# A two-layer decode kernel on one core: the last matmuls kept company by idle products, and one ninth of the gate's rows moved to 64 partitions and eight short transfers

## The chip, the core and the metric

The kernel runs on one NeuronCore of a Trainium2 chip. The metric is the device time of one execution in microseconds; the figure for a kernel is the median of several runs.

## What is computed

One token of two sequences (B = 2, model width D = 576) goes through attention over a cache, a gated MLP, the same attention once more and the same MLP once more. All arrays are float32, and both layers use the same weights and caches.

```python
B, Sq, D = 2, 1, 576
H, Sk, Dh = 32, 8192, 128          # k_cache, v_cache: (B, H, Sk, Dh)
Df = 4608                          # w_gate, w_up: (D, Df); w_down: (Df, D)
x = A_x
x = x + attention(layernorm(x))    # softmax(q k^T / sqrt(Dh)) v, then wo
x = x + mlp(layernorm(x))          # (gelu(x w_gate) * (x w_up)) w_down
x = x + attention(layernorm(x))
x = x + mlp(layernorm(x))
```

Each cache has 2 x 32 x 8192 x 128 values of 4 bytes, 268 MB in the units of the profile, and is read once per layer, apart from a few heads that stay in place from the first layer to the second. The three MLP matrices have 10.6 MB each and are read in both layers.

## The kernel before, in words

All loads go out from one engine, SyncE (SP in the profile), in an order that is written down in Python before any arithmetic: `plan_first`, `plan_mlp(0)`, `plan_second` and `plan_mlp(1)` append closures to one `queue`, and `pump` issues from its head as long as the head finds room. The room is one tile, `space`, of 50,176 float32 per partition, handed out by `Arena`. `done(key)` is called in the code behind the products that used a piece; it frees the piece's stretch and pumps again. The framework keeps eight semaphores for SP's transfers and goes round them, so that a transfer is issued only when the one eight places before it has landed; it may also wait for the engines that read its place before.

Attention (`attention`) goes over 62 items, each one batch and one or two heads: VectorE and GpSimd multiply the keys by the query, VectorE adds up, ScalarE makes the softmax, and TensorE multiplies by the values. In the second layer it goes through the items backwards and ends with eight pieces of `wo` (`project`, `out_rows`).

What the change touches is the second MLP, `mlp(1)`. Its weights are laid out as half rows. `half_rows` reads a matrix of 576 rows as 1152 half rows of 2304 values; partition p holds the nine half rows 9p to 9p + 8, called u = 0 to 8. A piece `us` of several u is one transfer. `GU` gives the pieces: before, the gate has three pieces of three u each (3456 KB a piece), the up matrix two pieces of three and three of one (1152 KB). `norm` lays the normalised x, transposed, in the tile `xt`, in nine blocks of 32 columns, block u matching half row u, with six columns of padding in front, so that `window(u, at)` can cut out eight columns of a block with the wanted columns shifted. `all_products` (L849) then accumulates for each u, each v of two and each c of four one product with 8 columns of `xt` held and 288 columns of weights moved.

`activate` (L858 to L871) turns the accumulated gate and up halves into `hT`: ScalarE, VectorE and again ScalarE in a chain of some ten small steps, once for v = 0 and once for v = 1. Behind it stand the products with the down matrix (L884). `DOWN[1]` gives its pieces: three of nine rows i (2592 KB), t = 0, 1 and 2, and the last nine rows, t = 3, as pieces of 3, 3, 2 and 1 (864, 864, 576, 288 KB). Each row i costs four products of 144 columns. In the records of the profile a float32 product appears twice, so that a nine-row piece has 72 records. `add_to_x` (L495) adds the sum to `x`, and four small transfers, two from SP and two from ScalarE's queue (L897), each of two partitions of 576 bytes, write the output.

Of the kernel before, what the change touches and what calls it, by code (L numbers as in the profile page):

```python
# [15 lines left out]
P = 128  # L16
# [24 lines left out]
NPLACE = 4  # L41
RING = 5 * SLOT
END = RING + NPLACE * PLACE
HELD = 5


# [76 lines left out]
def decode_layers(ctx, tc, x_in, kc, vc, wq, wo, wg, wu, wd, out):  # L123
# [97 lines left out]
    def half_rows(key, w, us, first):  # L221
# [6 lines left out]

        weights(key, len(us) * width, first, transfers)

    def split_rows(name, w, h, u):

        rows = w[:, DF // 2 * h:DF // 2 * (h + 1)].rearrange("(m r) w -> m r w", r=NU)

        def transfers(t):
            for e in range(2):
                nc.sync.dma_start(t[e::2, :], rows[:, 5 * e + u, :])

        weights((name, 0, h, u), DF // 2, None, transfers)
# [39 lines left out]
    def out_rows(layer, g):  # L279
# [12 lines left out]
    single = [range(u, u + 1) for u in range(NU)]  # L292
    three = [range(u, u + 3) for u in range(0, NU, 3)]
    WQ = [three, single]
    GU = [three, three[:-1] + single[-3:]]

    DOWN = [
        [[(t, i) for i in range(lo, lo + 4)] for t in range(NT) for lo in (0, 4)] + [[(t, NI - 1) for t in range(NT)]],
        [[(t, i) for i in range(NI)] for t in range(NT - 1)]
        + [[(NT - 1, i) for i in range(lo, hi)] for lo, hi in ((0, 3), (3, 6), (6, 8), (8, 9))],  # L300
    ]

    whole_at = (None, 0)
    def groups(layer):
# [70 lines left out]
    def plan_mlp(layer):  # L375
        if layer == 0:
            for h in range(2):
                for u in range(4):
                    split_rows("g", wg, h, u)
                split_middle(h)  # L380
                for u in range(4):
                    split_rows("u", wu, h, u)
        else:
            for g, (name, w) in enumerate((("g", wg), ("u", wu))):
                for us in GU[g]:
                    half_rows((name, layer, us[0]), w, us, 0)
        for rows in DOWN[layer]:
            down(layer, rows)

# [20 lines left out]
    diag = consts.tile([P, 4], F32, name="diag")  # L410
    of = consts.tile([P, B], F32, name="of")
    both = ident.rearrange("p (c v b r) -> p b r v c", c=4, v=4, b=B)[:, :, :, 0, :]
    eight = consts.tile([P, B, 4], F32, name="eight")
    nc.vector.reduce_sum(eight, both, axis=AX.X)
    nc.vector.tensor_add(diag, eight[:, 0, :], eight[:, 1, :])
    nc.vector.reduce_sum(of, eight, axis=AX.X)
# [18 lines left out]

    xt = consts.tile([P, PAD + NU * 32], F32, name="xt")
    nc.vector.memset(xt, 0.0)


# [17 lines left out]
        return smalls[0][0:p, 0:n]  # L459


    def norm(split=False):
        stats = work.tile([P, 6], F32, name="stats")
        nc.vector.bn_stats(stats, x)
        apart = work.tile([P, 4, 6], F32, name="apart")
        nc.vector.tensor_mul(
            apart, stats.unsqueeze(1).to_broadcast([P, 4, 6]), strip.unsqueeze(2).to_broadcast([P, 4, 6])
        )
        every4 = small(P, 4 * 6)
        nc.tensor.matmul(every4, same, apart.rearrange("p c t -> p (c t)"), start=True, stop=True)  # L470
        mv = work.tile([P, 2], F32, name="mv")
        nc.vector.bn_aggr(mv, every4)
        xc = once.tile([P, CW, 2], F32, name="xc", tag="xc")
        xr = x.rearrange("p (m r) -> p r m", r=NU)
        xs = xc.rearrange("p w s -> p (w s)")
        if split:
            xm = xs[:, :5 * 32].rearrange("p (u m e) -> p u m e", u=5, e=2)
            parts = [(xm[:, 0:4, :, e], xr[:, 5 * e:5 * e + 4, :], 0) for e in range(2)]
            parts += [(xm[:, 4, :, e], xr[:, 4, :], e) for e in range(2)]
            xs = xs[:, :5 * 32].rearrange("p (u q) -> p u q", u=5)  # L480
        else:
            parts = [(xc[:, :, s], x, s) for s in range(2)]
            xs = xs.rearrange("p (q u) -> p u q", u=NU)
        for to, of_x, s in parts:
            nc.vector.tensor_scalar(to, of_x, mv[:, 0:1], side[:, s:s + 1], op0=ALU.subtract, op1=ALU.mult)
        u = xs.shape[1]
        nc.vector.transpose(xt[:, PAD:PAD + 32 * u].rearrange("p (u q) -> p u q", u=u), xs)
        ve = work.tile([P, 1], F32, name="ve")
        nc.vector.tensor_scalar_add(ve, mv[:, 1:2], EPS)  # L489
        rstd = work.tile([P, 1], F32, name="rstd")  # L490
        nc.gpsimd.tensor_tensor(out=rstd, in0=ve, in1=mhalf, op=ALU.pow)  # L491
        return rstd
# [5 lines left out]
    def attention(layer):  # L498
# [314 lines left out]
            project(g)  # L813
        add_to_x()


    def mlp(layer):
        split = layer == 0
        rstd = norm(split)
        hT = once.tile([P, 2, NI, 2, 2, B], F32, name="hT", tag="xc")  # L820

        def window(u, at):

            return xt[:, PAD + 32 * u - at:PAD + 32 * u - at + 4 * B]

        def split_products(h):

            steps = [(("g", layer, h, u), u, 2, (0,)) for u in range(4)] + [(("gu", layer, h), 4, 1, (0, 1))]
            steps += [(("u", layer, h, u), u, 2, (1,)) for u in range(4)]
            for key, u, sides, gs in steps:  # L830
                w = ready.pop(key).rearrange("p (k c w) -> p k c w", c=4, w=HG)
                for k in range(2):
                    g, e = (k, 0) if u == 4 else (gs[0], k)
                    for c in range(4):
                        nc.tensor.matmul(  # L835
                            acc[32 * c:32 * c + 4 * B, h, :HG], window(u, 4 * g + 2 * e), w[:, k, c, :],
                            start=(key == steps[0][0] and k == 0), stop=(key == steps[-1][0] and k == 1),
                        )
                done(key)

        def all_products():

            for g, name in enumerate("gu"):
                for us in GU[g]:
                    w = ready.pop((name, layer, us[0])).rearrange("p (u v c w) -> p u v c w", v=2, c=4, w=HG)
                    for u in us:
                        for v in range(2):
                            for c in range(4):
                                nc.tensor.matmul(  # L849
                                    acc[32 * c:32 * c + 4 * B, v, :HG], window(u, 4 * g), w[:, u - us[0], v, c, :],  # L850
                                    start=(g == 0 and u == 0), stop=(g == 1 and u == NU - 1),
                                )
                    done((name, layer, us[0]))

        def activate(v):

            o = once.tile([P, 2, HG], F32, name="o", tag="row")
            nc.scalar.activation(o[:, 0, :], acc[:, v, :HG], AF.Copy, scale=rstd)  # L858
            gu = o[:, 1, :].rearrange("p (i r) -> p i r", i=NI)
            nc.vector.transpose(gu, o[:, 0, :].rearrange("p (m i) -> p i m", i=NI))  # L860
            g = gu[:, :, 0:4]
            a = once.tile([P, NI, 4], F32, name="ga", tag="part")
            nc.vector.tensor_mul(a, g, g)
            nc.vector.tensor_scalar(a, a, 0.044715, 1.0, op0=ALU.mult, op1=ALU.add)
            nc.vector.tensor_mul(a, a, g)
            nc.scalar.activation(a, a, AF.Tanh, scale=math.sqrt(2.0 / math.pi))
            nc.vector.scalar_tensor_tensor(a, a, 1.0, g, op0=ALU.add, op1=ALU.mult)
            nc.vector.tensor_mul(a, a, gu[:, :, 4:8])
            a, to = a.rearrange("p i (e b) -> p (i e) b", b=B), hT[:, v].rearrange("p i e s b -> p (i e) s b")
            nc.vector.tensor_scalar_mul(to[:, :, 0, :], a, 0.5)  # L870
            nc.scalar.mul(to[:, :, 1, :], a, 0.5)  # L871

        if not split:
            all_products()
        for v in range(2):
            if split:
                split_products(v)
            activate(v)
        for rows in DOWN[layer]:
            w = ready.pop(("d", layer, rows[0])).rearrange("p (i c) -> p i c", c=D)  # L880
            for k, (t, i) in enumerate(rows):
                v, e = divmod(t, 2) if split else (t % 2, t // 2)
                for c in range(4):
                    nc.tensor.matmul(  # L884
                        xps[32 * c:32 * c + 2 * B, :], hT[:, v, i, e, :, :].rearrange("p s b -> p (s b)"),
                        w[:, k, c * CW:(c + 1) * CW],
                        start=(rows is DOWN[layer][0] and k == 0), stop=(t, i) == (NT - 1, NI - 1),
                    )
            done(("d", layer, rows[0]))
        add_to_x()  # L890
# [2 lines left out]
    mlp(0)  # L893
    attention(1)
    mlp(1)
    for c in range(4):
        (nc.sync, nc.scalar)[c % 2].dma_start(  # L897
            out[:, :, c * CW:(c + 1) * CW].rearrange("b s d -> (b s) d"), x[32 * c:32 * c + B, :]
        )


# [25 lines left out]
```

## Time and profile before

| what | value |
|---|---|
| time, median of 3 runs | 2692.36 us (2692.12 to 2692.72) |
| time of the profiled execution | 2692.03 us |
| its span, first to last instruction | 2690.2 us |
| TensorE, VectorE, GpSimd busy | 917.2, 1851.0, 1213.9 us |
| bytes read from the chip's memory | 1153.18 MB |

All times inside the execution are microseconds from the start of the span. The span is 1.83 us shorter than the profiled execution's own time, and this execution was 0.33 us faster than the median. In a timeline row the first number is the start, the second the length from the first to the last instruction of the group, and the bracket says how long the engine had been idle before and what ended that. PE is TensorE, PEld its loads of held operands, DVE VectorE, ACT ScalarE, SPq and ACTq the issue of transfers from SyncE and ScalarE. In a row of stretches stand, for each engine, its busy time and its count of instructions, then the granted share of TensorE's clock, the mean busy share of the 16 DMA engines and what they moved in GB/s; a packet counts in the stretch in which it starts.

### The profile page before, as it was taken

How to read it: one execution, taken by the hardware profiler on the slowest of the kernel's cores; microseconds unless marked ns; L12 is line 12 of the kernel's file. 1: busy time of each engine (PE TensorE's matmuls, PEld its weight loads, DVE VectorE, ACT ScalarE, POOL GpSimd, SP SyncE). 2: the span in 40 equal slices, each digit the busy share in tenths (PEclk: the TensorE clock that was granted, in tenths of full speed). 3: DMA queues.
4: the chain of work that ended last, by engine and by line, in shares of the span. 5: the costliest groups of instructions: out<-in, count | busy, mean ns of one | idle time of the engine just before them, and what ended most of it. 6: DMA issues, size and time to landing. Idle time of an engine off the chain costs nothing.

```text
span 2690.2 us, 18178 instructions
## 1 busy us (share of the span) xinstructions
PE 917.2 (34%) x7020; PEld 300.9 (11%) x7020; DVE 1851.0 (69%) x1688; ACT 144.6 (5%) x736; POOL 1213.9 (45%) x550
## 2 busy tenths in 40 slices
PE   1323332332233233334654332233233323332355
PEld 0100010000001010111211110001010101010022
DVE  4877787678777776867028777777776877787740
ACT  0000000000000000000016000000000000000000
POOL 2644454454445444544018454445444544454420
PEclk7656656665666566666666665666566556656677
DMA  9999999999999999999999999999999999999998
GB/s 421 435 437 433 427 436 430 434 436 430 436 432 433 431 431 434 435 427 425 406 402 419 436 435 431 435 432 433 433 433 433 432 434 432 434 433 431 434 423 378
DMA packets 33687, 1154.36 MB, mean 429 GB/s; under 512 B 4008, under 2 KB 4032, under 8 KB 5824
## 3 DMA queue, kind: packets, MB, share of 16 engines
q1 hardware_dynamic: 33560, 1153.19, 99.7%
q8 instruction: 55, 0.90, 0.1%
q14 instruction: 32, 0.26, 0.0%
q10 hardware_dynamic: 40, 0.01, 0.0%
HBM read 1153.18 MB, written 0.00 MB: 429 GB/s over the span
## 4 chain that ended last, share of the span: by engine, by line
DMA 79%; PE 11%; DVE 7%; POOL 1%; ACT 1%; issue 1%; SPq 0%; ACTq 0%; POOLq 0%; DVEq 0%
DMA space<-in_A_k_cache_dram 40%; DMA space<-in_A_v_cache_dram 32%; PE acc L672 10%; DVE space L557 5%; DMA space<-in_B_w_down_dram 2%; DVE S L577 2%; DMA space<-in_B_w_gate_dram 2%; DMA space<-in_A_wo_dram 1%; DMA space<-in_B_w_up_dram 1%; POOL space L574 1%; DMA space<-in_A_wq_dram 1%; PE bank L884 0%; ACT space L567 0%; PE acc L835 0%; POOL space L561 0%
## 5 line engine op out<-in xcount | busy, mean ns | idle before, releaser
L574 POOL TENSOR_TENSOR space<-space 128x1024 f32<-128x1024 f32 (+1 forms) x510 | 1180.6, 2315 | 1207.8 <-DVE space L557 1197.0
L557 DVE TENSOR_TENSOR space<-space,bank 128x2048 f32<-128x2048 f32 (+1 forms) x512 | 1153.6, 2253 | 607.7 <-DMA space<-in_A_k_cache_dram 573.8
L672 PE MATMUL acc<-space,prz 128*8 128x512 f32 x4096 | 590.9, 740 | 451.9 <-DMA space<-in_A_v_cache_dram 447.8
L577 DVE TENSOR_REDUCE S<-space 128x16 f32<-128x1024 f32 (+1 forms) x512 | 609.8, 1191 | 3.5 <-POOL space L574 3.3
L525 PE MATMUL bank<-qsb,pick 4*64 4x128 f32 (+1 forms) x256 | 46.9, 439 | 780.2 <-DVE space L557 777.6
L672 PEld LDWEIGHTS acc<-space,prz 128*8 128x8 f32 x4096 | 118.5, 104 | 867.3 <-DMA space<-in_A_v_cache_dram 449.0
L629 ACT ACTIVATE nbs<-bank 64x1 f32<-64x1 f32 (+1 forms) x128 | 21.1, 165 | 2254.3 <-PE bank L608 2253.6
L525 PEld LDWEIGHTS bank<-qsb,pick 4*64 4x64 f32 (+1 forms) x256 | 21.1, 203 | 838.9 <-DVE space L557 807.7
L697 PE MATMUL bank<-of,osb 128*32 128x2 f32 x512 | 40.9, 202 | 130.8 <-DVE osb L688 130.8
L608 PE MATMUL bank<-m,unit 1*128 1x2 f32 (+1 forms) x136 | 39.2, 355 | 129.1 <-DVE m L606 129.1
L491 POOL TENSOR_TENSOR rstd<-ve,mhalf 128x1 f32<-128x1 f32 x4 | 2.2, 550 | 167.6 <-DVE ve L489 167.6
L688 DVE SCALAR_TENSOR_TENSOR osb<-acc,diag,osb 128x128 f32<-128x128 f32 x192 | 67.3, 351 | 6.8
L860 DVE STREAM_TRANSPOSE o<-o 128x288 f32<-128x288 f32 x4 | 2.8, 692 | 94.1 <-ACT o L858 94.1
L639 PE MATMUL bank<-sums,unit 128*128 128x2 f32 x120 | 35.2, 363 | 92.1 <-ACT prz L631 92.1
L631 ACT ACTIVATE prz<-S,nbs 64x128 f32<-64x128 f32 (+1 forms) x128 | 50.7, 396 | 12.4 <-POOL prz L621 8.3
L697 PEld LDWEIGHTS bank<-of,osb 128*32 128x32 f32 x512 | 35.7, 154 | 139.2 <-DVE osb L688 137.8
L600 PE MATMUL bank<-ident,m 128*1 128x128 f32 x68 | 25.0, 368 | 74.3 <-DVE m L598 74.2
L608 PEld LDWEIGHTS bank<-m,unit 1*128 1x128 f32 x136 | 33.3, 303 | 148.8 <-DVE m L606 148.8
L567 ACT ACTIVATE space<-space 128x128 f32<-128x128 f32 x164 | 48.3, 297 | 18.1 <-DVE space L557 16.1
L495 DVE TENSOR_TENSOR x<-bank,x 128x144 f32<-128x144 f32 x4 | 1.2, 307 | 67.8 <-PE bank L884 39.8
L561 POOL TENSOR_TENSOR space<-space,qs 128x512 f32<-128x512 f32 x24 | 30.4, 1270 | 27.1 <-ACT qs L556 25.6
L639 PEld LDWEIGHTS bank<-sums,unit 128*128 128x128 f32 x120 | 30.1, 311 | 97.2 <-ACT prz L631 97.2
(68 smaller groups left out, 380.0 us busy)
## 6 DMA issues: line engine op xcount, KB each, us to landing
space<-in_A_v_cache_dram SPq DMA_DIRECT2D x8, 4096.0 KB
space<-in_A_k_cache_dram SPq DMA_DIRECT2D x6, 4096.0 KB
space<-in_A_wo_dram SPq DMA_DIRECT2D x15, 1152.0 KB
space<-in_A_k_cache_dram SPq DMA_DIRECT2D x15, 1024.0 KB
space<-in_B_w_gate_dram SPq DMA_DIRECT2D x3, 3456.0 KB
space<-in_A_v_cache_dram SPq DMA_DIRECT2D x10, 1024.0 KB
space<-in_A_wq_dram SPq DMA_DIRECT2D x3, 3072.0 KB
space<-in_B_w_gate_dram SPq DMA_DIRECT2D x16, 576.0 KB
```

Of the source, the lines that this page charges most:

```text
L525: nc.tensor.matmul(qb[n][to, :], pick[32 * c:32 * c + 4, r:r + 1].to_broadcast([4, P // it.heads]), qsb[32 * c:32 * c + 4, (h % 4) * DH:(h ...
L557: nc.vector.tensor_tensor(out=u[:, :rows, :], in0=t[:, :rows, :], in1=qb[n].unsqueeze(1).to_broadcast([P, rows, DH]), op=ALU.mult)
L561: nc.gpsimd.tensor_tensor(out=u[:, rows:, :], in0=t[:, rows:, :], in1=q.unsqueeze(1).to_broadcast([P, JC - rows, DH]), op=ALU.mult,)
L567: nc.scalar.activation(u[:, j, :], u[:, j, :], AF.Copy, accum_out=S[n][:, k * JC + j:k * JC + j + 1])
L574: nc.gpsimd.tensor_tensor(out=half, in0=half, in1=u[:, :r, DH // 2:], op=ALU.add)
L577: nc.vector.tensor_reduce(out=S[n][:, k * JC:k * JC + own_rows(n, k)], in_=prod.pop((n, k)), axis=AX.X, op=ALU.add)
L608: nc.tensor.matmul(mT[n][:, :heads], ones[0:1, :], m1[:, :heads], start=True, stop=True)
L631: nc.scalar.activation(pr[at, lo:].rearrange("p (g e) -> p g e", e=4)[:, 0:it.rows // 2:2, :], s[at, :it.rows].rearrange("p (g r) -> p g r ...
L639: nc.tensor.matmul(tot[n][:, :ITEMS[n].heads], ones, rs.pop(n), start=True, stop=True)
L672: nc.tensor.matmul(accumulator(n)[32 * c:32 * c + 8, :], pr[:, at:at + 8], t[g // 4][:, g % 4 * 4:g % 4 * 4 + 4, :].rearrange("p j d -> p ...
L688: nc.vector.scalar_tensor_tensor(t, q[:, r, :], diag[:, r:r + 1], t, op0=ALU.mult, op1=ALU.add,)
L697: nc.tensor.matmul(po[lo:lo + 32, i, :], t[:, i::GH], of, start=True, stop=True)
```

## The change

It has four parts, all in the second MLP or behind it, apart from one small tile that changes its pool.

- The gate's ninth half rows (u = 8) no longer lie on 128 partitions. The piece is now `LOWER`, a range of u = 8 and 9: the half rows of partitions 0 to 63 lie as u = 8 on partitions 0 to 63, and those of partitions 64 to 127 as u = 9 beside them, on the same 64 partitions. Eight transfers bring it (`lower_rows`), each for eight partitions that lie four apart (two half rows each, 144 KB); two stand in the queue behind the first gate piece, three behind the second and three behind the third, which is now of two u. The matching x is one more block of 32 columns in `xt`, made by one more transpose in `norm`. The products with this piece are 16 over 64 partitions where they were 8 over 128.
- The down piece t = 2 comes as two pieces, of five and of four rows.
- Before each of the first five down pieces stand 4, 4, 2, 2 and 1 products of 288 columns that nothing reads (`idle_products`); they write to the tile `kept`, which is not used any more then.
- The output is written by two transfers of four partitions, one from SP and one from ScalarE's queue, where there were four of two partitions.

```diff
+LOWER = range(NU - 1, NU + 1)
...
+    def lower_rows(key, w, first):
+        width = w.shape[1] // 2
+        rows = w.rearrange("r (s w) -> (r s) w", w=width).rearrange("(e p u) w -> p e u w", e=2, u=NU)[:, :, NU - 1, :]
+        weights(key, 2 * width, first, lambda t: None)
+
+        def eighth(at):
+            def make():
+                nc.sync.dma_start(ready[key].rearrange("p (e w) -> p e w", w=width)[at], rows[at])
+                return True
+
+            return lambda: queue.append(make)
+
+        return [eighth(slice(lo + j, lo + 32, 4)) for lo in range(0, HALF, 32) for j in range(4)]
...
-    GU = [three, three[:-1] + single[-3:]]
+    GU = [three[:-1] + [range(6, 8), LOWER], three[:-1] + single[-3:]]
...
-        [[(t, i) for i in range(NI)] for t in range(NT - 1)]
+        [[(t, i) for i in range(NI)] for t in range(NT - 2)]
+        + [[(NT - 2, i) for i in range(lo, hi)] for lo, hi in ((0, 5), (5, 9))]
         + [[(NT - 1, i) for i in range(lo, hi)] for lo, hi in ((0, 3), (3, 6), (6, 8), (8, 9))],
+    IDLE = (4, 4, 2, 2, 1)
...
-            for g, (name, w) in enumerate((("g", wg), ("u", wu))):
-                for us in GU[g]:
-                    half_rows((name, layer, us[0]), w, us, 0)
+            short = iter(lower_rows(("g", layer, LOWER[0]), wg, 0))
+            for us, m in zip(GU[0], (2, 3, 3)):
+                half_rows(("g", layer, us[0]), wg, us, 0)
+                for _ in range(m):
+                    next(short)()
+            for us in GU[1]:
+                half_rows(("u", layer, us[0]), wu, us, 0)
...
-    eight = consts.tile([P, B, 4], F32, name="eight")
+    eight = once.tile([P, B, 4], F32, name="eight", tag="part")
...
-    xt = consts.tile([P, PAD + NU * 32], F32, name="xt")
+    xt = consts.tile([P, PAD + (NU + 1) * 32], F32, name="xt")
...
-    def norm(split=False):
+    def norm(split=False, lower=False):
...
+        if lower:
+            nc.vector.transpose(xt[:HALF, PAD + 32 * NU:], xs[HALF:, NU - 1, :])
...
+    def idle_products(n):
+        for _ in range(n):
+            nc.tensor.matmul(
+                kept.rearrange("p j d -> p (j d)")[0:4, :HG], ident[:, 0:4], xt[:, :HG], start=True, stop=True,
+            )
...
-        rstd = norm(split)
+        rstd = norm(split, lower=not split)
...
+                    k = HALF if us is LOWER else P
...
-                                    acc[32 * c:32 * c + 4 * B, v, :HG], window(u, 4 * g), w[:, u - us[0], v, c, :],
+                                    acc[32 * c:32 * c + 4 * B, v, :HG], window(u, 4 * g)[:k], w[:k, u - us[0], v, c, :],
...
-        for rows in DOWN[layer]:
+        for n, rows in enumerate(DOWN[layer]):
+            if layer == 1 and n < len(IDLE):
+                idle_products(IDLE[n])
...
-    for c in range(4):
-        (nc.sync, nc.scalar)[c % 2].dma_start(
-            out[:, :, c * CW:(c + 1) * CW].rearrange("b s d -> (b s) d"), x[32 * c:32 * c + B, :]
-        )
+    for b, engine in enumerate((nc.sync, nc.scalar)):
+        engine.dma_start(out[b, 0].rearrange("(c w) -> c w", c=4), x[b::32, :])
```

## Prediction

> **What bounds the kernel now.** I read the page first, then the timeline of the last 40 us, then the last microseconds in short stretches. From the page:
>
> ```profile
> span 2690.2 us, 18178 instructions
> ...
> DMA  9999999999999999999999999999999999999998
> GB/s 421 435 437 433 427 436 430 434 436 430 436 432 433 431 431 434 435 427 425 406 402 419 436 435 431 435 432 433 433 433 433 432 434 432 434 433 431 434 423 378
> ...
> q8 instruction: 55, 0.90, 0.1%
> q14 instruction: 32, 0.26, 0.0%
> q10 hardware_dynamic: 40, 0.01, 0.0%
> ```
>
> The 16 DMA engines are busy in every fortieth of the span, at about 430 GB/s; only the last slice falls. The bytes don't change, so the change can act only on what follows the last weights. That end, from the timeline:
>
> ```profile
> 2652.85 4.07 PE L849 MATMUL acc<-space,xt 128*8 128x288 f32 x64 [3.59 <-DMA space<-in_B_w_up_dram]
> 2658.42 1.16 PE L849 MATMUL acc<-space,xt 128*8 128x288 f32 x16 [1.50 <-DMA space<-in_B_w_up_dram]
> 2661.20 1.91 PE L849 MATMUL acc<-space,xt 128*8 128x288 f32 x16 [1.62 <-DMA space<-in_B_w_up_dram]
> ...
> 2667.41 3.98 PEld L884 LDWEIGHTS bank<-space,hT 128*4 128x4 f32 x72 [5.33 <-ACT o L858]
> 2667.44 4.44 PE L884 MATMUL bank<-space,hT 128*4 128x144 f32 x72 [4.33 <-DMA space<-in_B_w_down_dram]
> ...
> 2673.61 2.39 PE L884 MATMUL bank<-space,hT 128*4 128x144 f32 x72 [1.73 <-DMA space<-in_B_w_down_dram]
> ...
> 2679.74 7.31 PE L884 MATMUL bank<-space,hT 128*4 128x144 f32 x144 [3.74 <-DMA space<-in_B_w_down_dram]
> 2687.13 0.31 DVE L495 TENSOR_TENSOR x<-bank,x 128x144 f32<-128x144 f32 x1 [18.23 <-PE bank L884]
> 2687.47 0.91 SPq L897 DMA_DIRECT2D out_dram<-x  x2
> 2687.47 0.56 ACTq L897 DMA_DIRECT2D out_dram<-x  x2
> ```
>
> The same 72 records of a nine-row down piece take 4.44 us behind an idle time of 4.33 us and 2.39 us behind one of 1.73 us: 62 and 33 ns each. The last 144 start behind an idle time of 3.74 us and take 7.31 us, 51 ns each, so most of them run slowly. In short stretches:
>
> ```profile
> 2679.00:2680.00 1.00, 0.26 (x8) 0.17 (x12) 0.00 (x0) 0.00 (x0) 0.00 (x0) 0.50 0.90 371
> 2680.00:2681.00 1.00, 1.00 (x24) 0.63 (x20) 0.00 (x0) 0.00 (x0) 0.00 (x0) 0.50 0.78 323
> 2681.00:2682.00 1.00, 1.00 (x24) 0.63 (x20) 0.00 (x0) 0.00 (x0) 0.00 (x0) 0.50 0.68 283
> 2682.00:2683.00 1.00, 1.00 (x24) 0.60 (x18) 0.00 (x0) 0.00 (x0) 0.00 (x0) 0.50 0.58 240
> 2683.00:2684.00 1.00, 1.00 (x24) 0.59 (x16) 0.00 (x0) 0.00 (x0) 0.00 (x0) 0.50 0.55 226
> 2684.00:2685.00 1.00, 1.00 (x24) 0.61 (x19) 0.00 (x0) 0.00 (x0) 0.00 (x0) 0.50 0.42 166
> 2685.00:2685.50 0.50, 0.50 (x16) 0.37 (x12) 0.00 (x0) 0.00 (x0) 0.00 (x0) 0.65 0.17 65
> 2685.50:2686.00 0.50, 0.50 (x24) 0.40 (x19) 0.00 (x0) 0.00 (x0) 0.00 (x0) 1.00 0.12 33
> 2686.00:2687.00 1.00, 1.00 (x36) 0.58 (x24) 0.00 (x0) 0.00 (x0) 0.00 (x0) 1.00 0.00 0
> ```
>
> Two things stand here. The granted clock is 0.50 until about 2685 and 1.00 after it. And the DMA engines don't end together: 0.90 x 16 = 14 are busy at 2679.5, 9 at 2682.5, 7 at 2684.5, none with weights after about 2685.7. Summed, 0.10 + 0.22 + 0.32 + 0.42 + 0.45 + 0.58 + 0.42 = 2.5 us of all engines stay unused, so perfectly even loads would end 2.5 us sooner. TensorE is busy until 2687.05, some 1.3 us behind the last weights: weights and slow clock bind together.
>
> **The change part by part.** The sum is made against this execution (span 2690.2, own time 2692.03) and carried to the median 2692.36 by the 0.33 between them.
>
> *The ninth gate rows.* What a row costs is read from the starts of the pieces:
>
> ```profile
> 2620.07 4.97 PE L849 MATMUL acc<-space,xt 128*8 128x288 f32 x48 [5.44 <-DMA space<-in_B_w_gate_dram]
> 2628.18 5.95 PE L849 MATMUL acc<-space,xt 128*8 128x288 f32 x48 [3.14 <-DMA space<-in_B_w_gate_dram]
> 2636.39 3.90 PE L849 MATMUL acc<-space,xt 128*8 128x288 f32 x40 [2.27 <-DMA space<-in_B_w_gate_dram]
> ```
>
> A third of the distance of two three-row pieces is 8.21 / 3 = 2.74 us; the one-row up pieces lie 2661.20 - 2658.42 = 2.78 apart. So the row costs each of 16 engines 2.74 us. Each short transfer now covers eight partitions. If it uses eight engines, one partition each, these eight carry all the bytes: 2 x 2.78 = 5.56 us, 2.8 more than before, and the other eight 2.74 less. The end thus depends on which kind the last engine is.
>
> What makes an engine late? The landings in the second attention, at even spacing but for two:
>
> ```profile
> 2510.88 2.29 DVE L557 TENSOR_TENSOR space<-space,bank 128x2048 f32<-128x2048 f32 x1 [9.69 <-DMA space<-in_A_k_cache_dram]
> ...
> 2530.76 3.60 PE L672 MATMUL acc<-space,prz 128*8 128x512 f32 x16 [8.26 <-DMA space<-in_A_v_cache_dram]
> ...
> 2550.10 2.29 DVE L557 TENSOR_TENSOR space<-space,bank 128x2048 f32<-128x2048 f32 x1 [10.09 <-DMA space<-in_A_k_cache_dram]
> ...
> 2569.92 4.55 PE L672 MATMUL acc<-space,prz 128*8 128x512 f32 x28 [8.19 <-DMA space<-in_A_v_cache_dram]
> ```
>
> The distances are 19.88, 19.34 and 19.82. The DMA view of the stretches that end with the first and the third of these landings holds one fetch of instructions each, of two kinds:
>
> ```profile
> q8 instruction: 1, 0.02, 0.4%
> ...
> q14 instruction: 1, 0.01, 0.1%
> ```
>
> The middle one has none. So an engine that serves a fetch falls behind, it keeps its lag, and the last landing moves with it: by 19.82 - 19.34 = 0.48 us for the q14 one. Both kinds have hit the engine that is last. I followed the packets on each engine through the trace, which no view groups: the q8 fetches go round eight engines, the q14 fetches hit some of the other eight, and the engine that is last at the end is the one with most q14 fetches. Two engines alone take the two-partition loads of x (the eight loads and two of the output's writes are q10's 40 packets, four each: two with data, two that close), and they are of the second kind, one of them this late one. So I take it that the short transfers, being cut the same way, include the late engine: the last landing moves by +2.8 us. If they missed it, the move would be between -2.74 and about 0.
>
> [...] By a use of all 16 the term would be 0 instead of 2.8.
>
> *Queue and waits.* SP issues eight transfers more (eleven for gate rows instead of three, one more down piece, one write less; ScalarE's queue one write less). Eight semaphores go round, so the first up piece waits until the second gate piece has landed: about 2628.2 plus two short transfers on the late engine, 2 x 0.7, so 2629.6. Engines without short transfers then still hold the two-row piece, 2 x 2.74 us, until at least 2628.2 - 2 + 5.5 = 2631.7 (the late ones end within 2 us of the last in the stretches above). That leaves 2 us for the issue to take effect, with all later weights queued behind it on SP; I price it at 0 and treat the loss of this cover as a rival. The down pieces wait for products of gate rows and landings before 2645, well ahead of use.
>
> *Products.* A 288-column record takes 4.07 / 64 = 64 ns fast and, by the gate rows, 4.97 / 48 = 104 slow. The ninth row has 16 records more, 1.0 to 1.7 us, under the wait for the first up piece (over 2 us idle stand before each piece there). The 13 idle products have 26 records, 1.7 to 2.7 us in all: the first 8 (0.5 to 0.8) lie under the 5.33 us wait for `hT`, the next 8 under the 1.73 us one, the rest under waits for pieces. They end long before the pieces land, so they cost nothing; uncovered, a group would cost up to 0.8. The second transpose on VectorE lies in the 5.44 us that TensorE waits for the first gate piece.
>
> *Clock and split.* With t = 2 in two parts, TensorE starts 4 x 2.78 / 4 = 2.8 us sooner on the first five rows (a nine-row down piece has 2592 KB, a row 288), and every wait between pieces falls below 2 us. The trace has speed kept behind 1.73 and lost behind 3.74; I take it as kept. Fast, the last 144 records need 144 x 33 = 4.8 us, spread over pieces that land one after another, so TensorE waits for the last piece, whose 8 records take 0.27 (slow 0.5) plus the length of one record, some 0.3. Where 1.4 us lie now between the last weights (2685.7) and VectorE's add (2687.13), about 0.8 will: -0.6, between -0.9 and 0.
>
> *Output.* Each queue loses one of two issues: half of 0.91 and of 0.56, so -0.3 to -0.45; I take -0.4, bounds -0.5 and 0 (four partitions could take longer than two).
>
> Sum: +2.8 - 0.6 - 0.4 = +1.8 us. 2692.03 + 1.8 + 0.33 = **2694.2 us**. The lag of the late engine may differ by a fetch or two and the clock may fall: 2693.0 to 2695.5 for this case alone.
>
> **The rivals.** *All eight short-transfer engines end early.* For: seven of 16 are done by 2682.5, early enough to take 2.8 us more and still end at about 2685.3 at the latest; the late ones then end 2.74 us sooner. Against: the packets as I followed them. Last weights near 2685.3 instead of 2685.7: -0.4 - 0.6 - 0.4 = -1.4, 2690.9 us, faster. It decides if the engine that is last is not among the eight.
>
> *The short transfers are spread over all 16 engines.* The landing stays; -0.6 - 0.4 = -1.0, 2691.4 us. Two partitions on two engines speak against it.
>
> *Idle products don't keep the clock.* The first case with its last 8 records slow and all five pieces of the end at 62 ns: +0.6, 2694.8, inside its range.
>
> *Slots run dry.* If an issue takes more than the 2 us of cover, all engines without short transfers stand still before the first up piece. From the issue of the output (2687.47) to the end of the span, 2.7 us pass for a whole small transfer; if nothing overlapped, eight short ones at 2.7 less their own 0.7 would cost 16 us, and one group of three 6 us: 2694.2 + 6 = 2700 us. Against: the one-row up pieces land 2.78 apart, no more than a third of a large piece, so transfers follow each other without a gap.
>
> [...]
>
> **How the numbers follow.** Late engine included 0.62 (with the clock's rival in it); not included 0.17; spread over 16 0.09; slots dry 0.07; something unseen 0.05. The range from 2690.6 to 2696.0 holds the first three and leaves out the slots and the unseen. Within 0.2% (5.4 us, about what a measurement can tell from no change) lie all but the last two: same 0.86, slower 0.10, faster 0.04; the most that even loads, clock and output could give is 2.5 + 0.9 + 0.5 = 3.9 us, below 5.4.
>
> **What would show it.** Landing: in the stretches, few engines (one or two, shares near 0.1) busy until about 2688.5, where now seven are busy until 2685. If the first rival holds, the shares fall later and more steeply and end before 2685.5. Clock: granted 1.00 from the second down piece to the end, and the last records at 33 ns. Queue: the DMA share stays near 1.00 from 2625 to 2645; a dip there is the slots' rival. Output: one issue on each queue. I'd be wrong in kind if the last weights moved by less than a microsecond.

## The result, and the profile after

The changed kernel takes **2712.22 us** (median of six runs, 2711.04 to 2713.21); the kernel before took 2692.54 us beside it (six runs, 2691.25 to 2693.84). The ratio is 1.0073, 95% interval 1.0062 to 1.0084: 19.7 us slower, where 1.8 us were forecast. The profiled execution took 2711.36 us with a span of 2709.6 us.

The page of the changed kernel, its rows of DMA and its row of the add-up of the keys (busy time, mean ns of one, idle time before it and what ended most of that):

```profile
span 2709.6 us, 18275 instructions
...
DMA  9999999999999999999999999999999999999978
GB/s 421 431 434 434 434 434 433 434 433 433 433 433 432 433 433 433 433 431 416 417 396 429 433 433 432 434 432 433 433 434 433 434 432 434 434 433 433 428 304 377
...
L607 DVE TENSOR_REDUCE S<-space 128x16 f32<-128x1024 f32 (+1 forms) x512 | 610.0, 1192 | 43.8 <-DMA space<-in_B_w_gate_dram 41.7
```

The slice before the last (about 2574 to 2642 us) has fallen to 304 GB/s; the slice before the last had 423 in the kernel before. The last row is odd: the add-up works on keys, yet 41.7 us of its idle time end with a transfer of the *gate*. Stretches of 5 us of the changed kernel (the columns are those of the prediction; the last three are granted clock, busy share of the DMA engines and GB/s):

```profile
2610.00:2615.00 5.00, 0.00 (x0) 0.00 (x0) 0.00 (x0) 0.00 (x0) 0.00 (x0) 0.50 0.96 409
2615.00:2620.00 5.00, 0.00 (x0) 0.00 (x0) 0.00 (x0) 0.00 (x0) 0.00 (x0) 0.50 0.35 147
2620.00:2625.00 5.00, 0.86 (x3) 0.57 (x3) 1.79 (x3) 0.00 (x0) 0.00 (x0) 0.50 0.02 9
2625.00:2630.00 5.00, 1.85 (x15) 1.10 (x19) 1.78 (x7) 1.31 (x6) 0.00 (x0) 0.50 0.00 0
2630.00:2635.00 5.00, 5.00 (x40) 1.60 (x36) 0.00 (x0) 0.00 (x0) 0.00 (x0) 0.76 0.00 0
2635.00:2640.00 5.00, 3.35 (x40) 1.23 (x35) 1.40 (x4) 0.00 (x0) 0.00 (x0) 1.00 0.97 354
```

From 2617 on only a few DMA engines still move weights, the last packet ends at 2621.6, and then nothing moves until 2635. The unused share is (0.65 + 0.98 + 1.00 + 1.00 + 0.03) x 5 = 18.3 us, nearly the whole loss. The kernel before had no such gap:

```profile
2615.00:2620.00 5.00, 0.00 (x0) 0.00 (x0) 1.32 (x4) 0.00 (x0) 0.55 (x1) 0.50 0.99 426
2630.00:2635.00 5.00, 4.12 (x36) 1.07 (x28) 0.00 (x0) 0.00 (x0) 0.00 (x0) 0.59 1.00 431
```

What stopped the transfers is read from the timeline of the changed kernel around the gap:

```profile
2570.68 8.84 PE L702 MATMUL acc<-space,prz 128*8 128x512 f32 x64 [7.77 <-DMA space<-in_A_v_cache_dram]
...
2579.20 1.22 DVE L607 TENSOR_REDUCE S<-space 128x16 f32<-128x1024 f32 x1
...
2593.06 0.33 SPq L228 DMA_DIRECT2D space<-in_B_w_gate_dram  x1
2595.85 3.46 SPq L243 DMA_DIRECT2D space<-in_B_w_gate_dram  x2
2622.17 1.22 DVE L607 TENSOR_REDUCE S<-space 128x16 f32<-128x1024 f32 x1 [41.75 <-DMA space<-in_B_w_gate_dram]
2623.42 0.29 DVE L628 TENSOR_REDUCE m<-S 128x1 f32<-128x128 f32 x1
...
2629.33 8.52 PE L702 MATMUL acc<-space,prz 128*8 128x512 f32 x61
2634.44 0.34 SPq L228 DMA_DIRECT2D space<-in_B_w_gate_dram  x1
```

Read it from the bottom. The second gate piece is issued at 2634.44, after products with the values (L702) had given up its place. Those products need the softmax, which needs the maximum (L628), which needs the last add-up of the keys. VectorE stands still before that add-up from 2580.4 to 2622.17, until the first two short transfers, issued at 2595.85, have landed. In the kernel before, the same add-up waited 1.39 us for GpSimd, and the gate's three pieces went out from 2592.34 on, the second of them at 2595.12:

```profile
2580.63 1.22 DVE L577 TENSOR_REDUCE S<-space 128x16 f32<-128x1024 f32 x1 [1.39 <-POOL space L574]
2592.34 5.89 SPq L227 DMA_DIRECT2D space<-in_B_w_gate_dram  x3
```

In the view of the waits of the changed kernel (us in all, times, longest) these are two rows, one of VectorE and one of SP:

```profile
DVE S L607 <- DMA space<-in_B_w_gate_dram: 41.7, 1, 41.7
```

```profile
SPq L228 <- PE acc L702: 33.0, 1, 33.0
```

Nothing in the computation asks for the wait of the add-up. But in the built program the add-up does carry it, for the semaphores of both transfers, which stand ahead of it because `done` of the part of the keys before pumps the queue. The first of them and the add-up there, as [step, count] in values (a partition of `space` has 50,176):

```
SP  transfer  writes space at 35072  [200704, 8] [2304, 2] [1, 2304]
DVE add-up    reads  space at 47104  [50176, 128] [128, 16] [1, 64]
```

The transfer writes 4608 columns from 35,072 on, in eight partitions that lie four apart; the add-up reads columns from 47,104 on. They share no value; as two flat runs of addresses they do cross. That the framework compares flat runs where a step is not one partition is an inference. In e1_contig below the step is one partition, and the add-up carries no such wait, although the flat runs cross there as well.

The tail, by contrast, looks as forecast:

```profile
2692.11 2.39 PE L923 MATMUL bank<-space,hT 128*4 128x144 f32 x72 [0.19 <-DMA space<-in_B_w_down_dram]
...
2704.93 1.14 PE L923 MATMUL bank<-space,hT 128*4 128x144 f32 x24 [1.52 <-DMA space<-in_B_w_down_dram]
2706.14 0.31 DVE L525 TENSOR_TENSOR x<-bank,x 128x144 f32<-128x144 f32 x1 [19.48 <-PE bank L923]
2706.47 0.60 SPq L936 DMA_DIRECT2D out_dram<-x  x1
2706.48 0.63 ACTq L936 DMA_DIRECT2D out_dram<-x  x1
```

```profile
2700.00:2702.00 2.00, 0.92 (x24) 0.54 (x24) 0.00 (x0) 0.00 (x0) 0.00 (x0) 1.00 0.79 317
2702.00:2704.00 2.00, 0.92 (x24) 0.54 (x24) 0.00 (x0) 0.00 (x0) 0.00 (x0) 1.00 0.38 147
2704.00:2706.00 2.00, 1.03 (x24) 0.43 (x24) 0.00 (x0) 0.00 (x0) 0.00 (x0) 1.00 0.04 14
```

The second down piece runs at 2.39 / 72 = 33 ns a record, the clock is 1.00 from there to the last products, and each queue issues one output write.

### The profile page after: what moved, and what is told of

Read it like the earlier page. It is cut to its first block, busy times and chain, and to the rows that moved or that the text cites. A ratio compares the mean times of both kernels' runs of the same rounds, so it can differ in the third digit from the quotient of the medians.

```text
span 2709.6 us, 18275 instructions
## 1 busy us (share of the span) xinstructions
PE 918.4 (34%) x7062; PEld 299.3 (11%) x7062; DVE 1851.5 (68%) x1689; ACT 144.7 (5%) x736; POOL 1214.8 (45%) x550
## 4 chain that ended last, share of the span: by engine, by line
DMA 78%; PE 12%; DVE 8%; POOL 1%; issue 1%; ACT 1%; SPq 0%; ACTq 0%; DVEq 0%; POOLq 0%
DMA space<-in_A_k_cache_dram 39%; DMA space<-in_A_v_cache_dram 31%; PE acc L702 10%; DVE space L587 5%; DVE S L607 2%; DMA space<-in_A_wo_dram 2%; DMA space<-in_B_w_up_dram 2%; DMA space<-in_B_w_down_dram 2%; DMA space<-in_B_w_gate_dram 2%; POOL space L604 1%; DMA space<-in_A_wq_dram 1%; PE acc L871 0%; ACT space L597 0%; PE bank L755 0%; DMA x<-in_A_x_dram 0%
## 5 line engine op out<-in xcount | busy, mean ns | idle before, releaser
L702 PE MATMUL acc<-space,prz 128*8 128x512 f32 x4096 | 595.6, 745 | 450.3 <-DMA space<-in_A_v_cache_dram 446.2
L607 DVE TENSOR_REDUCE S<-space 128x16 f32<-128x1024 f32 (+1 forms) x512 | 610.0, 1192 | 43.8 <-DMA space<-in_B_w_gate_dram 41.7
L702 PEld LDWEIGHTS acc<-space,prz 128*8 128x8 f32 x4096 | 118.2, 104 | 870.2 <-DMA space<-in_A_v_cache_dram 448.7
```

The source lines that it names most:

```text
L607: nc.vector.tensor_reduce(out=S[n][:, k * JC:k * JC + own_rows(n, k)], in_=prod.pop((n, k)), axis=AX.X, op=ALU.add)
L702: nc.tensor.matmul(accumulator(n)[32 * c:32 * c + 8, :], pr[:, at:at + 8], t[g // 4][:, g % 4 * 4:g % 4 * 4 + 4, :].rearrange("p j d -> p ...
```

## The experiments

Two questions: is the false wait the whole loss, and do the other terms of the sum hold? All eight kernels are edits of the changed kernel.

| kernel | short transfers | median, us | ratio to before, 95% interval |
|---|---|---|---|
| before | none | 2692.2 | |
| changed | 8 x 8, four apart, 2/3/3 | 2712.22 | 1.0073 (1.0062 to 1.0084) |
| e1_contig | 8 x 8 neighbours, 2/3/3 | 2707.81 | 1.0058 (1.0045 to 1.0071) |
| e2_no_lower | none | 2692.59 | 1.0002 (0.9994 to 1.0011) |
| e3_later | 8 x 8, four apart, 0/4/4 | 2694.82 | 1.0010 (1.0001 to 1.0019) |
| e4_one | one of 64 neighbours, 0/0/1 | 2701.95 | 1.0037 (1.0024 to 1.0051) |
| e5_hold | as changed, held until the keys are gone | 2695.01 | 1.0010 (1.0001 to 1.0019) |
| e6_eight_apart | 8 x 8, eight apart, 0/4/4 | 2707.83 | 1.0062 (1.0050 to 1.0075) |
| e7_sixteen | 4 x 16, four apart, 0/2/2 | 2699.16 | 1.0026 (1.0017 to 1.0036) |
| e8_half | 4 x 8, four apart, half of the rows, 0/2/2 | 2692.01 | 1.0001 (0.9992 to 1.0009) |

(0/4/4: so many short transfers in the queue behind the first, second and third gate piece. The kernel before had 2692.21 us beside the first four experiments and 2692.2 beside the last four.)

### e1_contig: the stepping taken away

```diff
-        return [eighth(slice(lo + j, lo + 32, 4)) for lo in range(0, HALF, 32) for j in range(4)]
+        return [eighth(slice(lo, lo + 8)) for lo in range(0, HALF, 8)]
```

> The changed kernel, but each short transfer covers eight partitions in a row instead of eight that lie four apart; same bytes, same eight transfers, same places in the queue. Theory A (the last add-up of the keys waits for the first two short transfers because their stepping over partitions makes the framework take them for writes into the keys' place): no such wait, weights flow without a pause, 2692 to 2695 us, with the late engine's landing some 2.8 us later than before and 2694.2 the likeliest. Rival B (the eight extra transfers use up the eight semaphores and the queue runs dry): nothing changes, 2711 to 2713 us. Rival C (short transfers are slow in themselves): 2711 to 2713 us as well.

Measured 2707.81 us. The false wait is gone: the last add-up starts at 2580.30, where it waits 1.40 us for GpSimd only. Yet only 4 us come back, so the time was a miss, and something new stands in its place. Stretches of this kernel:

```profile
2615.00:2620.00 5.00, 0.00 (x0) 0.00 (x0) 1.82 (x6) 0.00 (x0) 0.55 (x1) 0.50 1.04 334
2620.00:2625.00 5.00, 2.37 (x21) 0.82 (x25) 0.00 (x0) 0.00 (x0) 0.00 (x0) 0.50 0.99 376
2625.00:2630.00 5.00, 2.18 (x32) 0.73 (x24) 0.00 (x0) 0.00 (x0) 0.00 (x0) 0.94 0.94 289
2630.00:2635.00 5.00, 0.00 (x0) 0.00 (x0) 0.00 (x0) 0.00 (x0) 0.00 (x0) 0.74 0.86 251
2635.00:2640.00 5.00, 4.07 (x43) 1.39 (x46) 0.00 (x0) 0.00 (x0) 0.00 (x0) 0.57 0.93 256
```

The DMA engines are busy, at shares of 0.86 to 1.04, but they move 250 to 380 GB/s in place of 430. They don't wait for an issue; their packets take longer: those of 9216 bytes had medians of 0.45 to 0.57 us between 2610 and 2650, where they took 0.35 us, and never more than 0.36, in the changed kernel between 2585 and 2655. So the layout that brings the wait also keeps the transfers fast; which feature of it does so is the question of e4, e6 and e7.

### e2_no_lower: the other three parts alone

```diff
-    GU = [three[:-1] + [range(6, 8), LOWER], three[:-1] + single[-3:]]
+    GU = [three, three[:-1] + single[-3:]]
...
-            short = iter(lower_rows(("g", layer, LOWER[0]), wg, 0))
...
+            for g, (name, w) in enumerate((("g", wg), ("u", wu))):
+                for us in GU[g]:
+                    half_rows((name, layer, us[0]), w, us, 0)
```

> The changed kernel with the gate's ninth rows back on 128 partitions in the three-row piece; idle products, the split of t = 2 and the two output writes stay. Theory A: all of the loss lies in the short transfers, and the rest is worth what was forecast for it, -0.6 and -0.4: 2691.5 us, between 2690.9 and 2692.5. Rival D (the idle products or the split cost the 20 us): 2711 us or some part of it.

Measured 2692.59 us: the idle products, the split piece and the two output writes together are not told apart from no change (the interval is -1.6 to +3.0 us; the -1.0 us forecast for them lies inside it). To within that interval the loss is wholly in the lower rows.

### e3_later: the short transfers behind the last add-up

```diff
-            for us, m in zip(GU[0], (2, 3, 3)):
+            for us, m in zip(GU[0], (0, 4, 4)):
```

> The changed kernel, with partitions four apart as in the change, but no short transfer behind the first gate piece, four behind the second and four behind the third. These come after the last add-up in the program. Theory A: the add-up no longer waits, 2692 to 2696 us. Rivals B and C: 2711 us, since the same transfers still go out.

Measured 2694.82 us, as the theory had it. The last add-up starts at 2580.44. The tail in stretches of this kernel has the shape that the prediction described for a landing moved on few engines:

```profile
2683.00:2684.00 1.00, 1.00 (x33) 0.79 (x26) 0.00 (x0) 0.00 (x0) 0.00 (x0) 1.00 0.40 164
2684.00:2685.00 1.00, 0.58 (x9) 0.10 (x8) 0.00 (x0) 0.00 (x0) 0.00 (x0) 1.00 0.32 122
2685.00:2686.00 1.00, 0.82 (x24) 0.44 (x19) 0.00 (x0) 0.00 (x0) 0.00 (x0) 1.00 0.17 71
2686.00:2687.00 1.00, 0.01 (x1) 0.01 (x3) 0.00 (x0) 0.00 (x0) 0.00 (x0) 1.00 0.18 71
2687.00:2688.00 1.00, 0.91 (x24) 0.53 (x24) 0.00 (x0) 0.00 (x0) 0.00 (x0) 1.00 0.15 62
2688.00:2689.00 1.00, 0.60 (x16) 0.32 (x16) 0.00 (x0) 0.00 (x0) 0.00 (x0) 1.00 0.06 23
```

Three engines (0.17 x 16) still work between 2685 and 2688, and one on average between 2688 and 2689. The kernel without short transfers, e2_no_lower, ends otherwise:

```profile
2685.00:2686.00 1.00, 0.40 (x16) 0.08 (x4) 0.00 (x0) 0.00 (x0) 0.00 (x0) 1.00 0.56 226
2686.00:2687.00 1.00, 0.44 (x16) 0.39 (x20) 0.00 (x0) 0.00 (x0) 0.00 (x0) 1.00 0.36 134
2687.00:2688.00 1.00, 0.51 (x20) 0.18 (x16) 0.00 (x0) 0.00 (x0) 0.00 (x0) 1.00 0.13 51
```

Nine engines (0.56 x 16) work there between 2685 and 2686, so the end is more even. By their packets the last weights land at 2688.18 in e2_no_lower and at 2688.62 in e3_later. That is only 0.4 us apart, because the profiled execution of e2_no_lower took 2694.30 us, 1.7 above its median, while that of e3_later is its median. The size of the move therefore rests on the medians, not on these two landings.

### e4_one: one transfer of 64 partitions

```diff
-        return [eighth(slice(lo + j, lo + 32, 4)) for lo in range(0, HALF, 32) for j in range(4)]
+        return [eighth(slice(0, HALF))]
...
-            for us, m in zip(GU[0], (2, 3, 3)):
+            for us, m in zip(GU[0], (0, 0, 1)):
```

> The changed kernel, but the ninth gate rows come to the lower 64 partitions in one transfer of 64 partitions (four for each of 16 engines) behind the two-row gate piece. Theory A: no wait, and no engine gets more than before: the landing as before, 2691.5 us, between 2690.9 and 2692.5, 2 to 3 us below the kernel with short transfers over partitions in a row. If short transfers spread over all 16 engines anyway, the two are equal.

Measured 2701.95 us, a miss again, with no false wait (the add-up starts at 2581.20) and with the slow stretch of e1 in a purer form:

```profile
2625.00:2630.00 5.00, 0.84 (x16) 0.22 (x12) 0.00 (x0) 0.00 (x0) 0.00 (x0) 1.00 1.02 348
2630.00:2635.00 5.00, 4.66 (x48) 1.51 (x40) 0.00 (x0) 0.00 (x0) 0.00 (x0) 0.66 1.03 229
2635.00:2640.00 5.00, 0.00 (x0) 0.00 (x0) 0.00 (x0) 0.00 (x0) 0.00 (x0) 0.78 1.01 218
2640.00:2645.00 5.00, 4.00 (x32) 1.06 (x32) 0.00 (x0) 0.00 (x0) 0.00 (x0) 0.54 0.99 251
```

All engines are busy (shares of 0.99 to 1.03), and from 2630 on little more than half of the usual 430 GB/s moves (218 to 251). From 2610 to 2650 e4_one has 345 GB/s on average and e3_later 421; at 432 GB/s the difference is worth 7.0 us, and the two times lie 7.1 us apart. The packets of the trace (no view groups them; I sorted them by size and by the stretch in which they start) say the same, in us, median and upper tenth:

```
kernel          stretch      9216 B          18432 B         27648 B
before          2620-2625    -               -               1.03  1.03
e3_later        2625-2630    0.35  0.35      0.69  0.69      1.03  1.03
e4_one          2630-2635    0.72  0.74      1.40  1.42      1.84  2.00
e4_one          2635-2640    0.71  0.73      1.36  1.41      2.03  2.10
e6_eight_apart  2620-2625    0.71  0.72      1.00  1.40      1.07  2.10
e7_sixteen      2625-2630    0.65  0.71      1.26  1.36      1.43  1.93
```

In e4 every size takes about twice its time (0.71 us for 0.35, 1.36 to 1.40 for 0.69, 1.84 to 2.03 for 1.03). Whether that takes neighbouring partitions in one transfer, or comes without them as well, is asked by e6 and e7.

The packets also tell how many engines a transfer uses. By the counts, each transfer leaves one packet of 4 bytes on every engine that it uses: 16 for a piece on 128 partitions (4009 in the kernel before, 4025 in e2_no_lower, which has one down piece more and no short transfer), two for each two-partition transfer of the prediction's queue q10 (20 for ten). The whole run has 4089 of them in the changed kernel and in e1, e3, e5 and e6, 4041 in e4, 4089 in e7 and 4057 in e8: eight for each transfer of eight partitions, and 16 for one of 64 or 16 partitions.

### e5_hold: the same queue, the same step, the wait alone taken away

```diff
             def make():
+                if any(isinstance(c, tuple) and isinstance(c[0], tuple) and c[0][0] == "k" for c in arena.live):
+                    return False
                 nc.sync.dma_start(ready[key].rearrange("p (e w) -> p e w", w=width)[at], rows[at])
```

> The changed kernel with one condition more: a short transfer is issued only once no keys of the attention are left in the arena. The queue keeps its order (two, three, three), the short transfers stay four partitions apart, and they still stand in the middle of the gate's pieces; only they come behind the last add-up of the keys in the program, so that the add-up no longer waits for them. Theory 'false wait' (the add-up held up by the first two short transfers costs all that the change lost beyond its landing): the last add-up (L607) runs near 2580 and not at 2622, the DMA share stays near 1.0 from 2605 to 2640, and the time is that of the later placement, 2693 to 2697 us. Rival 'slots' (many short transfers in the middle of the queue block it by themselves): a dip of the DMA share between 2605 and 2640 stays, and the time is 2705 to 2712 us.

Measured 2695.01 us. The order of the queue is the changed kernel's, with two short transfers behind the first gate piece; they only stand behind the last add-up in the program. Of this kernel, the add-up (now in line 609) in the timeline, and the stretches that were empty:

```profile
2580.42 1.22 DVE L609 TENSOR_REDUCE S<-space 128x16 f32<-128x1024 f32 x1 [1.41 <-POOL space L606]
```

```profile
2615.00:2620.00 5.00, 0.62 (x2) 0.50 (x2) 2.15 (x7) 0.00 (x0) 0.55 (x1) 0.50 1.01 431
2620.00:2625.00 5.00, 4.64 (x40) 1.62 (x44) 0.00 (x0) 0.00 (x0) 0.00 (x0) 0.50 0.98 414
2625.00:2630.00 5.00, 1.34 (x16) 0.29 (x12) 0.00 (x0) 0.00 (x0) 0.00 (x0) 0.84 0.91 387
2630.00:2635.00 5.00, 4.40 (x48) 1.35 (x40) 0.00 (x0) 0.00 (x0) 0.00 (x0) 0.72 0.95 376
```

So the wait is worth 2712.22 - 2695.01 = 17.2 us, and the rival of the slots is refuted: eight short transfers in the middle of this queue don't run it dry once the add-up is ahead of them (busy shares of 0.91 to 1.01 between 2615 and 2635). Some 0.7 us of the share are missing from 2625 to 2635, within the spread of the time.

### e6_eight_apart and e7_sixteen: what makes the packets slow

```diff
-        return [eighth(slice(lo + j, lo + 32, 4)) for lo in range(0, HALF, 32) for j in range(4)]
+        return [eighth(slice(j, HALF, 8)) for j in range(8)]
...
-            for us, m in zip(GU[0], (2, 3, 3)):
+            for us, m in zip(GU[0], (0, 4, 4)):
```

> The short transfers behind the second and third gate piece (four and four), each of eight partitions that lie eight apart over all 64, none of them neighbours. [...] Rival 'neighbours' (only directly neighbouring partitions in flight at once are slow): packets stay at 0.35 us, and the time is that of the four-apart pieces at this place, 2693 to 2696.5 us.

```diff
-        return [eighth(slice(lo + j, lo + 32, 4)) for lo in range(0, HALF, 32) for j in range(4)]
+        return [eighth(slice(j, HALF, 4)) for j in range(4)]
...
-            for us, m in zip(GU[0], (2, 3, 3)):
+            for us, m in zip(GU[0], (0, 2, 2)):
```

> Four transfers of 16 partitions four apart in place of eight of eight, two behind the second and two behind the third gate piece. If a transfer of 16 partitions uses 16 engines, the bytes lie even on all engines again. [...] Rival 'neighbours' (four apart is far enough): packets stay at 0.35 us, the landing doesn't move, and the time is that of the kernel without lower rows, 2691 to 2693.5 us.

Measured 2707.83 and 2699.16 us; the packets are in the table above. In neither kernel does a transfer hold direct neighbours, and in both the packets of 9216 bytes reach twice their time (medians of 0.71 and 0.65 us, upper tenths of 0.72 and 0.71, for 0.35), so the "neighbours" are refuted as the condition. What the fast kernels (e3, e5, e8) have, and e1, e4, e6 and e7 have not, is that a short transfer takes eight partitions four apart within a span of 32. By what the others are slowed, no run shows.

For both my estimate was 2698 to 2703 us, with packets at twice their time as in e4. The time of e7 lies in it. For e6 the estimate was made of 16 packets on the late engine with 0.35 us more each, 5.6 us on top of e3_later's 2694.8, and it missed the size: it counts the short packets alone, and the long ones are stretched as well, 27,648 bytes to a median of 1.59 and an upper tenth of 2.0 us between 2640 and 2645, where they took 1.03 in the kernel before.

How far the packets are stretched differs: in e1 those of 9216 bytes, at medians of 0.45 to 0.57 us between 2610 and 2650, had an upper tenth of up to 0.72, and the longest took 0.94, less than three times 0.35. Why their medians are below the 0.71 us of e4 stays open.

### e8_half: half of the late engine's load taken away

```diff
-        return [eighth(slice(lo + j, lo + 32, 4)) for lo in range(0, HALF, 32) for j in range(4)]
+        return [eighth(slice(j, 32, 4)) for j in range(4)]
...
-            for us, m in zip(GU[0], (2, 3, 3)):
+            for us, m in zip(GU[0], (0, 2, 2)):
```

> This kernel leaves out half of the ninth gate rows: only partitions 0 to 31 of the 64 are loaded, by four short transfers four apart, two behind the second and two behind the third gate piece; the products run over 64 partitions as before. Theory 'late engine' (the eight engines of the short transfers include the one that ends last, so its landing moves with their bytes): against the eight short transfers at this place (2694.8 us) each of the eight engines has 8 packets of 0.35 us less, 2.8 us, so 2691 to 2693 us. Rival 'all bytes count' (the stream ends with the sum of bytes): 590 KB less at 430 GB/s are 1.4 us, 2693.4 us. Rival 'the landing of other engines decides': no change, 2694 to 2696 us.

This kernel leaves out half of the ninth gate rows, so it doesn't compute the whole gate; it tells only what the bytes cost. Measured 2692.01 us, 2.8 us below e3_later; the 1.4 us of the bytes alone would have given 2693.4. This speaks for the late engine, though the intervals of both kernels are some 2 us to either side and don't settle it by themselves.

No kernel tried is told apart from the one before as faster. By these runs none of this kind would be: where the short transfers were fast and complete (e3, e5) the kernel was 2.6 to 2.8 us slower, and without them the rest is worth nothing that could be measured.

## Why the prediction was wrong

**Where it failed: "Queue and waits", priced at 0.** The step asked what SP waits for, and closed with the sentence that the down pieces wait for products and landings before 2645. It never asked who waits for the new transfers. The change put two of them ahead of the last add-up of the keys in the program, and their step of four partitions gave the add-up a wait. With it the softmax, the products with the values and the place for the second gate piece came some 39 us late (2634.44 in place of 2595.12): 33.0 us of SP's waiting, 18.3 us of dry DMA engines, 17.2 us of time between the changed kernel and e5_hold. So the term that was put at 0 measured 17.2 us. It could have been seen beforehand, since the wait stands in the built program.

**The slots' rival** named the right sign, a dip of the DMA share from 2625 to 2645, with a wrong cause. The dip came, from 2617 to 2635; e5_hold has the same queue and no such dip.

**The ninth gate rows, +2.8 us.** Right in mechanism as far as the runs show it, and near in size: e3_later stands 2.2 us above e2_no_lower, and e8_half 2.8 below e3_later, each with an interval of some 2 us to either side. No row that the step had shows eight engines for eight partitions; it took them from the two-partition loads of x. The counts of 4-byte packets bear it out (64 more for eight transfers, 4089 against 4025 in e2_no_lower), which refutes the rival of all 16. That the late engine is among the eight fits the tail of e3_later and the time of e8_half, and isn't shown more directly. What the step did not see is that their speed hangs on which partitions are written together (0.35 us for a packet of 9216 bytes in the changed kernel and e3, medians of 0.45 to 0.72 in e1, e4, e6 and e7); this cost nothing in the layout as changed, and 4.3 to 13.0 us in the other layouts at later places (e7 and e6 against e3).

**Clock and split, -0.6 us.** Right in the profiled executions: from the last weights (by their packets) to VectorE's add it was 1.60 us before (2685.53 to 2687.13) and is 1.02 after (2705.12 to 2706.14), 0.98 in e3_later. The median of e2_no_lower doesn't show it, being 0.4 us above the kernel before. Which of the two, the split or the idle products, holds the clock was not separated: every kernel run has both.

**Output, -0.4 us.** Wrong in sign, and small: the issue on SP did fall from 0.91 to 0.60 us, but that on ScalarE's queue, taken at half of 0.56, is 0.63 for a single write, and from VectorE's add to the end of the span it takes 2709.6 - 2706.14 = 3.5 us where it took 2690.2 - 2687.13 = 3.1; in e2, e3, e5 and e8 it was 3.2 to 3.4. So about +0.3 in place of -0.4, by single executions.

**Idle products.** Right that they cost nothing on the path, wrong in length: the first eight records take 2.10 us after the change, 0.26 each, where 0.064 to 0.104 was taken from the gate's records. In the changed kernel the first group did not keep the clock: TensorE still waited 3.18 us before the first down piece, which took 3.56 us (49 ns a record), and the granted clock was 0.50 from 2687 to 2690. From 2691 on it was 1.00, and the pieces behind the idle products still waited for transfers. In e3_later the first down piece took 2.39 us (33 ns a record), and the clock was 1.00 in every stretch from 2678 to 2691, so what the first group does for the clock stays open.

Put together with these sizes, and without the wait, the sum is +2.2 to +2.8, -0.6 and +0.3, that is +1.9 to +2.5 us; e5_hold measured +2.8 and e3_later +2.6. (The first term is itself taken from e3_later, so this shows that the terms fit together and is no second proof.) The forecast of 2694.2 us was thus one for a kernel without the false wait: e5_hold's 2695.01 lies in the range of 2693.0 to 2695.5. That it comes so near is in part luck: the output came out 0.7 us worse than forecast, and the first term, at 2.2 by e3_later and e2_no_lower, 0.6 better.

## What to carry to other kernels

When transfers move ahead in a queue, look in the built program at the waits of every engine that reads the same tile, not only at the waits of the engine that issues; here a transfer that steps over partitions held up a read of other columns for 41.7 us. Then ask which partitions are written at the same moment: a full busy share of the DMA engines was no proof of a full rate (1.01 at 218 GB/s in e4_one, 1.01 at 431 in e3_later), and the GB/s beside it told the difference. And where a few engines end last, count the engines that a narrow transfer uses (here eight for eight partitions, by the 4-byte packets): if the late ones are among them, its bytes may move the end, as e8_half suggests, which took 2.8 us less than e3_later with half of these bytes.

## What was not expected of the hardware

- Busy shares near 1.0 at half the rate: 218 to 251 GB/s in e4_one between 2630 and 2645, with packets of 9216 bytes at 0.71 us in place of 0.35; e3_later writes the same bytes by eight transfers of eight partitions four apart at 394 to 431 GB/s between 2625 and 2640.
- Partitions eight apart are no better: e6_eight_apart, without neighbours in any transfer, took as long (2707.83 us) as e1_contig with neighbours alone (2707.81), though its short transfers stand later in the queue.
- Idle products of 288 columns took, in the changed kernel, 0.26 to 0.28 us a record (2.10 us for 8, 1.13 for 4) at a granted clock of 1.00, four times a record of `all_products` at the same width and clock (0.064 us in the kernel before, from 2652.85 on). Whether their four held columns, or that all of them write the same place, is the reason was not tried.
